# Batch 0's first loads cut at another place and put in another order, and its key-value products in one row

## The chip, the cores and the metric

The kernel runs on one core of a Trainium2 chip. What counts is the device time of one execution in microseconds. A core has five engines that work side by side, each through its own list of instructions: TensorE (PE; its weight loads stand as PEld), VectorE (DVE), ScalarE (ACT), GpSimd (POOL) and SyncE (SP, here only an issuer of transfers). Sixteen DMA engines move the data between the chip's main memory and the core's memory of 128 partitions.

## The reference

A linear attention over 8 batches, 8 heads, 576 tokens and 64 dimensions, with an RMS norm, feeds a mixture of 8 experts with soft slots (4 slots for each). All data are 32-bit floats.

```
kv  = einsum('bhsd,bhse->bhde', k, v)          # one 64x64 matrix per batch and head
out = einsum('bhsd,bhde->bhse', q, kv)
x   = out / sqrt(mean(out*out) + 1e-6) * g_norm    # 4608 tokens x 512
logits = x @ phi                                # 4608 x 32 slots
d = softmax(logits over tokens);  slot_input = d.T @ x
h = relu(slot_input[e] @ w1[e]);  slot_out[e] = h @ w2[e]      # 8 experts, 512x1024 and 1024x512
result = softmax(logits over slots) @ slot_out
```

Inputs are read once: keys, values and queries (28 MB) and the weights (34 MB); 9.4 MB are written.

## The kernel before, in words

Every operation is recorded first, with its engine, by a small planner (class `Order`), and then emitted in the recorded order for each engine; the planner only adds the waits. So the order of the calls in the function is the order of each engine's list, and all compute instructions show the planner's line, 215.

**Memory.** Loads go into one large array, `arena`: 144 columns at its head (phi and the norm's weights) and behind them a field of 160 blocks of 256 columns. `KV_AT`, `Q_AT` and `W_AT` give each piece its block. Batch 0's keys and values have block 0 (4608 columns: two halves of heads, `g` = 0 and 1, each 2048 columns of `kv_main` and 256 of `kv_rest`). Directly behind, at block 18, stands the q of batches 0 and 1 (`Q_AT[0]`): 2048 columns of `q_main` for batch 0, 2048 for batch 1, 512 of `q_rest` for the token tile that both share. Blocks are used again: the fourth batch's keys and values go to block 0 once batch 0's products have read it.

**Loads.** All go out on SP's queue, in order. Before, the first is the head and half `g` = 0 of batch 0; the second the half `g` = 1 and batch 0's `q_main`; the third batch 1's keys and values; the fourth the rest of that q; the fifth batch 2's keys and values with the next q. They are issued without any wait. The next three follow behind batch 0's products in the program, and the first of them waits until block 0 is free. Later loads (the last attention data, the experts' weights) are issued behind certain token tiles or experts, each when its place is free. The stores of the result use the same queue at the end.

**Attention.** `Kv` has for each batch `products` (64-column matmuls), `borders` (the last 64 tokens, and the copy of the products to `kvT` on ScalarE) and `slots` (transposes, the product with the norm-weighted phi, and the copies to `bd`, which is the weight side of what follows). For batch 0 the two halves of heads are worked off one after the other. Then the 36 token tiles (`T`) go by: `products(T)` multiplies q by `bd` on TensorE; ScalarE squares and evicts; VectorE and GpSimd norm, sum and scale. Batch 1's keys and values are multiplied (`kv_step(1, 0)`, `kv_step(1, 1)`) on TensorE right before tile 3, and its slots fall into tile 3; batch 2's come at tile 8 and before, and so on.

**Fills.** `fill` and `fill_wide` are matmuls whose result is never read. `EARLY` says how many stand at the start: five short ones (`fill`, 16-bit zeros, 512 columns), two wide ones (`fill_wide`, 32-bit ones, 512 columns) ahead of batch 0, one short in each half, and two wide ones behind the first half.

**Experts and output.** The softmax over tokens ends in `sTe`; then eight experts run, `expert_h` with `w1` and `expert_y` with `w2`, each behind its weights' loads, and the output is made in twelve chunks: chunks 0 to 5 behind the first half of the experts' second product, chunks 6 to 11 behind the second. The last store takes chunks 8 to 11 (3072 KB), the one before it chunks 6 and 7 (1536 KB).

Of the kernel before, what the change touches and what calls it, by code (L numbers as in the profile page):

```python
# [5 lines left out]
F32 = mybir.dt.float32  # L6
# [5 lines left out]
P = 128  # L12
B, H, S, D = 8, 8, 576, 64
# [9 lines left out]
CT = 12  # L23
NCH = NT // CT
NX = 14
EARLY = (5, 2, 0)
LATE_FILL = (4, 3, 3, 1, 1)
TOK = 4608
UNIT = 4096
# [3 lines left out]
KV_AT = (0, 36, 54, 0, 90, 126, 18, 54)  # L33
Q_AT = (18, 72, 108, 36)
# [27 lines left out]
SHARED = (5, 11)  # L62
BEHIND = {4: (2, 3), 5: (4, 5, 6, 7)}
HEAD = 144
SCRATCH = 1024
WORK = {
    "kvT": (1, 256), "sq": (2, 1024), "part": (3, 512), "ms": (3, 16), "r0": (2, 16), "r": (3, 16), "r1": (2, 16),
# [221 lines left out]
def soft_moe_linear_attention(nc, first_in, kv0_in, kv_in, q0_in, kv2_in, kv4_in, kv5_in, t3_in, w_in, out):  # L289
# [3 lines left out]
    wk = Pool({tag: [nc.sbuf([P, n], F32, f"{tag}{i}") for i in range(bufs)] for tag, (bufs, n) in WORK.items()})  # L293
    banks = nc.psum(8)
    arena = const.tile([P, HEAD + ARENA], F32, name="arena")
    phi_sb = arena[:, :128].rearrange("p (g w n) -> p g w n", g=2, w=2)
# [5 lines left out]
    def place(at, n):  # L302
        return arena[:, HEAD + at * KB : HEAD + at * KB + n]

    def load_row(at, src):
        nc.sync.dma_start(place(at, src.shape[-1]), src)
# [4 lines left out]
    def kv_rest(b, g):  # L311
        return place(KV_AT[b], TOK)[:, g * 2304 + 2048 : g * 2304 + 2304]
# [28 lines left out]
        return parts[k][:, at : at + 256]  # L341


    nc.sync.dma_start(arena[:, : HEAD + 2304], first_in)
    load_row(KV_AT[0] + 9, kv0_in)
    load_row(KV_AT[1], kv_in[0])
    load_row(Q_AT[0] + 8, q0_in)
    load_row(KV_AT[2], kv2_in)


# [47 lines left out]
    def pool(**tags):  # L398
        return Pool({tag: [flat_banks(banks, b, n) for b in at] for tag, (n, *at) in tags.items()})

    ps = pool(o=(2, 0, 2), kv=(2, 4), m=(1, 6), s=(1, 7))


    class Kv:
# [10 lines left out]
        def products(self, r):  # L415
            g, w = divmod(r, 2)
            main = kv_main(self.b, g).rearrange("p (r w c n) -> p r w c n", r=2, w=2, c=4)
            for c in range(4):
                for i in range(2):
                    lo = 64 * i  # L420
                    nc.tensor.matmul(
                        self.pkv[lo : lo + 64, w, g],
                        lhsT=main[:, w, 1, c, lo : lo + 64],
                        rhs=main[:, w, 0, c, lo : lo + 64],
                        start=c == 0 and (g == 0 or self.b == 0),
                        stop=False,
                    )

        def borders(self, gs):

            for g in gs:
                half = kv_rest(self.b, g).rearrange("p (w n) -> p w n", w=2)
                for i in range(2):
                    for w in range(2):
                        lo, at = 64 * i, 64 * w
                        nc.tensor.matmul(
                            self.pkv[lo : lo + 64, w, g],
                            lhsT=half[at : at + 64, 1, lo : lo + 64],
                            rhs=half[at : at + 64, 0, lo : lo + 64],
                            start=False,  # L440
                            stop=g == gs[-1],
                        )
            n = len(gs)
            self.kvT = wk.tile([P, n, 2, D], F32, tag="kvT", name=f"kvT{self.b}_{gs[0]}", bufs=1)
            nc.scalar.copy(self.kvT, self.pkv[:, :, gs[0] : gs[0] + n].rearrange("p w g d -> p g w d"))

        def slots(self, gs):
# [211 lines left out]
    first = {b: 9 * (b // 2) + 4 * (b % 2) for b in range(B)}  # L659
# [8 lines left out]
    def kv_step(b, i):  # L668
        if i == 0:
            kvs[b] = Kv(b)  # L670
            kvs[b].products(0)
            kvs[b].products(1)
        elif i == 1:
            kvs[b].products(2)
            kvs[b].products(3)
            kvs[b].borders((0, 1))
        else:
            kvs[b].slots((0, 1))
# [9 lines left out]
    def fill(n, cols=256, home=None):  # L688

        if not n:  # L690
            return
        t = home if home is not None else ps.tile([P, 2, 512], F32, tag="o", name="fill", bufs=2)[:, 1]
        for i in range(n):
            nc.tensor.matmul(
                t[:, :cols].rearrange("p (a n) -> p a n", n=256),
                lhsT=zeros[:, :P],
                rhs=zeros.unsqueeze(1).to_broadcast([P, cols // 256, 256]),
                start=True,
                stop=True,
            )  # L700

    def fill_wide(t, n):
        for i in range(n):
            nc.tensor.matmul(
                t.rearrange("p (a n) -> p a n", n=P),
                lhsT=ones,
                rhs=ones.unsqueeze(1).to_broadcast([P, 4, P]),
                start=True,
                stop=True,
            )  # L710

    fill(EARLY[0], cols=512)
    fill_wide(ps.tile([P, 512], F32, tag="m", name="fill"), 2)

    for g in range(2):
        kv = Kv(0, "o" if g else "kv", 2 if g else None)
        kv.products(2 * g)
        kv.products(2 * g + 1)
        kv.borders((g,))
        fill(1, cols=512)  # L720
        kv.slots((g,))
        fill_wide(ps.tile([P, 512], F32, tag="m", name="fill"), EARLY[1 + g])
    load_row(KV_AT[3], kv_in[1])
    load_row(Q_AT[1] + 8, kv4_in)
    load_row(Q_AT[2], kv5_in)
# [1 line left out]
    for T in range(NT - 2):  # L727
# [4 lines left out]
        o = products(T, (lambda: kv_step(late[0], 2)) if late else None)  # L732
# [110 lines left out]
    ps = pool(y=(2, 0), m=(2, 2, 4, 6))  # L843
# [182 lines left out]
def build_program():  # L1026
    import concourse.bacc as bacc

    nc = bacc.Bacc("TRN2", target_bir_lowering=False, num_devices=1, dynamic_dma_scratch_size=SCRATCH)
    shapes = {  # L1030
        "first": (P, HEAD + 2304), "kv0": (P, 2304 + 2048), "kv": (2, P, TOK), "q0": (P, 2560),
        "kv2": (P, TOK + 2048),
        "kv4": (P, 2560 + TOK), "kv5": (P, 2 * TOK), "t3": (P, 3 * TOK),
        "w": (1, 2 * NE * P * UNIT),
    }
    args = [nc.dram_tensor(f"in_{n}_dram", s, F32, kind="ExternalInput").ap() for n, s in shapes.items()]
    args.append(nc.dram_tensor("out_0_dram", (1, 4 * NCH * P * 4 * CT * NS), F32, kind="ExternalOutput").ap())
    order = Order(nc)
    soft_moe_linear_attention(order, *args)
    order.emit()  # L1040
    return nc
# [62 lines left out]
```

## Time and profile before

| | |
|---|---|
| runs (device us) | 171.58, 171.75, 244.36; median 171.75 |
| profiled execution | 171.73 us, its span 170.4 us |
| busy in the span | PE 151.0, PEld 104.0, DVE 86.9, ACT 88.5, POOL 59.6 us |
| moved | 71.65 MB, 421 GB/s over the span |

The time of an execution is a little longer than its span, which runs from the first to the last instruction. Busy time is the time in which an engine has an instruction at work. A transfer has an issue (on SP's list), packets on the sixteen DMA engines, and a landing, when the waiting engines may go on. The share of DMA is the mean busy share of the sixteen engines; packets that overlap in the records can carry it a little above 1.

### The profile page before, as it was taken

How to read it: one execution, taken by the hardware profiler on the slowest of the kernel's cores; microseconds unless marked ns; L12 is line 12 of the kernel's file. 1: busy time of each engine (PE TensorE's matmuls, PEld its weight loads, DVE VectorE, ACT ScalarE, POOL GpSimd, SP SyncE). 2: the span in 40 equal slices, each digit the busy share in tenths (PEclk: the TensorE clock that was granted, in tenths of full speed). 3: DMA queues.
4: the chain of work that ended last, by engine and by line, in shares of the span. 5: the costliest groups of instructions: out<-in, count | busy, mean ns of one | idle time of the engine just before them, and what ended most of it. 6: DMA issues, size and time to landing. Idle time of an engine off the chain costs nothing.

```text
span 170.4 us, 4234 instructions
## 1 busy us (share of the span) xinstructions
PE 151.0 (89%) x1834; PEld 104.0 (61%) x1834; DVE 86.9 (51%) x185; ACT 88.5 (52%) x230; POOL 59.6 (35%) x73
## 2 busy tenths in 40 slices
PE   7998998999999899999899989989999989989200
PEld 3457987979688888796696664345566533454000
DVE  1111437743677265763936798724888036319300
ACT  3015778786965887768849864202234044418300
POOL 7000247757356755366482589300000004000000
PEclk9999999999999999999999999999999999999855
DMA  5999999999999999999999999999999999999996
GB/s 193 440 435 417 478 413 409 457 430 478 419 415 439 432 441 413 419 400 460 400 458 408 448 408 423 431 458 396 431 427 431 452 435 396 427 415 439 415 447 288
DMA packets 3933, 71.65 MB, mean 421 GB/s; under 512 B 742, under 2 KB 742, under 8 KB 874
## 3 DMA queue, kind: packets, MB, share of 16 engines
q1 hardware_dynamic: 3562, 71.18, 97.8%
q8 instruction: 14, 0.23, 0.5%
q0 software_dynamic: 352, 0.20, 0.4%
q14 instruction: 5, 0.04, 0.1%
HBM read 61.94 MB, written 9.44 MB: 419 GB/s over the span
## 4 chain that ended last, share of the span: by engine, by line
PE 54%; DMA 16%; ACT 15%; DVE 6%; issue 1%; SPq 0%
PE psum L215 54%; DMA arena<-in_w_dram 10%; DMA arena<-in_kv_dram 6%; ACT bd L215 4%; ACT sq L215 4%; ACT xall L215 2%; DVE ms L215 2%; DVE logits L215 1%; ACT part L215 1%; ACT arena L215 1%; ACT r L215 1%; ACT d L215 1%; DVE part L215 1%; DVE acc L215 1%; DVE r L215 0%
## 5 line engine op out<-in xcount | busy, mean ns | idle before, releaser
L215 PE MATMUL psum<-bd,arena 128*128 128x192 f32 (+1 forms) x320 | 56.6, 336 | 2.4 <-ACT bd L215 1.2
L215 PEld LDWEIGHTS psum<-bd,arena 128*128 128x128 f32 (+1 forms) x320 | 45.5, 179 | 9.7 <-ACT xall L215 3.5
L215 DVE TENSOR_REDUCE ms<-sq 128x16 f32<-128x1024 f32 (+1 forms) x19 | 22.1, 1162 | 28.6 <-ACT sq L215 28.5
L215 POOL TENSOR_TENSOR part<-part,r 128x512 f32<-128x512 f32 x17 | 17.8, 1047 | 48.9 <-DVE r L215 48.9
L215 POOL TENSOR_TENSOR xall<-xall,r 128x512 f32<-128x512 f32 x34 | 34.7, 1042 | 0.0
L215 ACT ACTIVATE sq<-psum 128x512 f32<-128x512 f32 x36 | 21.5, 596 | 9.0 <-PE psum L215 8.9
L215 PEld LDWEIGHTS psum<-arena 128*64 128x64 f32 (+1 forms) x640 | 18.8, 137 | 6.6 <-issue 3.0
L215 PE MATMUL psum<-arena 128*64 128x64 f32 (+1 forms) x640 | 21.4, 226 | 0.3 <-DMA arena<-in_kv_dram 0.3
L215 ACT COPY xall<-psum 128x512 f32<-128x512 f32 x34 | 20.7, 608 | 0.0
L215 ACT COPY part<-psum 128x256 f32<-128x256 f32 (+1 forms) x38 | 13.7, 359 | 9.2 <-DVE part L215 8.0
L215 DVE TENSOR_REDUCE logits<-part 128x64 f32<-128x512 f32 (+1 forms) x18 | 17.8, 991 | 0.0
L215 PE MATMUL psum<-arena,xall 128*32 128x256 f32 x256 | 15.0, 380 | 0.4 <-DMA arena<-in_w_dram 0.4
L215 DVE COPY arena<-psum 128x768 f32<-128x768 f32 (+1 forms) x12 | 10.5, 889 | 6.8 <-PE psum L215 6.8
L215 ACT COPY arena<-psum 128x768 f32<-128x768 f32 (+1 forms) x14 | 10.2, 754 | 7.1 <-PE psum L215 7.1
L215 PE MATMUL psum<-logits,part 32*128 32x384 f32 x96 | 12.7, 527 | 0.6 <-ACT arena L215 0.4
L215 POOL DMA_DIRECT2D out_dram<-arena x2 | 1.2, 589 | 33.8 <-DVE arena L215 33.8
L215 PE MATMUL psum<-arena,sq 128*32 128x256 f32 x224 | 12.7, 379 | 0.2 <-DVE sq L215 0.2
L215 PEld LDWEIGHTS psum<-arena,xall 128*32 128x32 f32 x256 | 8.1, 110 | 6.9 <-issue 1.4
L215 PE MATMUL psum<-xall,d 128*32 128x258 f32 x144 | 10.8, 390 | 1.0 <-ACT d L215 1.0
L215 ACT COPY bd<-psum 64x128 f32<-64x128 f32 (+1 forms) x32 | 9.8, 308 | 2.4 <-PE psum L215 2.2
L215 PEld LDWEIGHTS psum<-arena,sq 128*32 128x32 f32 x224 | 7.2, 110 | 5.1 <-DVE sq L215 0.5
L215 ACT COPY kvT<-psum 128x256 f32<-128x256 f32 (+1 forms) x9 | 3.1, 348 | 12.6 <-PE psum L215 12.5
(80 smaller groups left out, 129.7 us busy)
## 6 DMA issues: line engine op xcount, KB each, us to landing
arena<-in_w_dram SPq DMA_DIRECT2D x4, 4096.0 KB, 23.8
arena<-in_w_dram SPq DMA_DIRECT2D x4, 2048.0 KB, 20.5
arena<-in_t_dram SPq DMA_DIRECT2D x1, 6912.0 KB, 35.6
arena<-in_w_dram SPq DMA_DIRECT2D x2, 3072.0 KB, 22.9
arena<-in_kv_dram SPq DMA_DIRECT2D x2, 2304.0 KB, 19.0
arena<-in_kv_dram SPq DMA_DIRECT2D x1, 4608.0 KB, 40.3
arena<-in_kv_dram SPq DMA_DIRECT2D x1, 3584.0 KB, 29.9
arena<-in_kv_dram SPq DMA_DIRECT2D x1, 3328.0 KB, 26.0
```

The lines of the kernel that those rows point to most:

```text
L215: inst = getattr(engine, method)(*args, **kwargs)
```

## The change

The same bytes come in four transfers again, cut at other places. The first one holds the head and the start of batch 0's keys and values, 512 columns (2048 bytes a row). The second holds the rest of batch 0's keys and values, both halves, 4240 columns. The third is the whole q of batches 0 and 1, 4608 columns, and the fourth batch 1's keys and values. Ahead of batch 0 stand now five short fills, five wide and one short. Batch 0's products are worked off in one row: the first half's products, half of the second's, then the slots of the first half, the rest of the second, its slots, and one wide fill. The copy `kvT` of a half goes to its own part of the tile.

```diff
-EARLY = (5, 2, 0)
+EARLY = (5, 5, 1, 1)
+AHEAD = 512
-    nc.sync.dma_start(arena[:, : HEAD + 2304], first_in)
-    load_row(KV_AT[0] + 9, kv0_in)
+    nc.sync.dma_start(arena[:, :AHEAD], first_in)
+    nc.sync.dma_start(arena[:, AHEAD : HEAD + TOK], kv0_in)
+    load_row(Q_AT[0], q0_in)
     load_row(KV_AT[1], kv_in[0])
-    load_row(Q_AT[0] + 8, q0_in)
     load_row(KV_AT[2], kv2_in)
...
-            self.kvT = wk.tile([P, n, 2, D], F32, tag="kvT", name=f"kvT{self.b}_{gs[0]}", bufs=1)
+            self.kvT = wk.tile([P, 2, 2, D], F32, tag="kvT", name=f"kvT{self.b}_{gs[0]}", bufs=1)[:, gs[0] : gs[0] + n]
...
     fill(EARLY[0], cols=512)
-    fill_wide(ps.tile([P, 512], F32, tag="m", name="fill"), 2)
-
-    for g in range(2):
-        kv = Kv(0, "o" if g else "kv", 2 if g else None)
+    wide = ps.tile([P, 512], F32, tag="m", name="fill")
+    fill_wide(wide, EARLY[1])
+    fill(EARLY[2], home=wide, cols=512)
+
+    halves0 = [Kv(0, "o" if g else "kv", 2 if g else None) for g in range(2)]
+    for g, kv in enumerate(halves0):
         kv.products(2 * g)
+        if g:
+            halves0[0].slots((0,))
         kv.products(2 * g + 1)
         kv.borders((g,))
-        fill(1, cols=512)
-        kv.slots((g,))
-        fill_wide(ps.tile([P, 512], F32, tag="m", name="fill"), EARLY[1 + g])
+    halves0[1].slots((1,))
+    fill_wide(ps.tile([P, 512], F32, tag="m", name="fill"), EARLY[3])
     load_row(KV_AT[3], kv_in[1])
...
-        "first": (P, HEAD + 2304), "kv0": (P, 2304 + 2048), "kv": (2, P, TOK), "q0": (P, 2560),
+        "first": (P, AHEAD), "kv0": (P, HEAD + TOK - AHEAD), "kv": (2, P, TOK), "q0": (P, TOK),
```

The host lays the input arrays out to match; nothing else is changed.

## Rows read from the trace of the kernel before

**Rows 1.** The page: busy time by engine, and strips of 40 slices in tenths.
```profile
PE 151.0 (89%) x1834; PEld 104.0 (61%) x1834; DVE 86.9 (51%) x185; ACT 88.5 (52%) x230; POOL 59.6 (35%) x73
...
PEclk9999999999999999999999999999999999999855
DMA  5999999999999999999999999999999999999996
```

**Rows 2.** Busy time by stage: stretch, engines, granted TensorE clock, DMA share, GB/s.
```profile
0.00:1.76 1.76, 0.70 (x2) 0.28 (x3) 0.58 (x3) 1.02 (x1) 0.88 (x8) 1.00 0.00 0
1.76:3.00 1.24, 1.24 (x4) 0.55 (x3) 0.15 (x1) 0.26 (x1) 1.03 (x3) 1.00 0.87 205
3.00:5.00 2.00, 2.00 (x4) 0.86 (x4) 0.00 (x0) 0.00 (x0) 1.10 (x4) 1.00 1.03 436
30.00:60.00 30.00, 29.12 (x406) 24.71 (x408) 17.72 (x37) 23.07 (x64) 18.29 (x18) 1.00 1.02 437
...
158.80:160.50 1.70, 0.00 (x0) 0.00 (x0) 0.55 (x1) 0.48 (x1) 0.00 (x0) 1.00 1.00 426
160.60:162.00 1.40, 0.00 (x0) 0.00 (x0) 0.00 (x0) 0.00 (x0) 0.00 (x0) 0.50 1.05 448
```

**Rows 3.** Waits of PE: total us, times, longest us.
```profile
PE psum L215 <- DMA arena<-in_w_dram: 0.4, 1, 0.4
```

**Rows 4.** Order of time on SP's list (start, us): first issues, last two stores.
```profile
0.74 0.38 SPq L215 DMA_DIRECT2D arena<-in_first_dram  x1
...
1.18 0.42 SPq L215 DMA_DIRECT2D arena<-in_kv_dram  x1
...
1.64 0.43 SPq L215 DMA_DIRECT2D arena<-in_kv_dram  x1
2.12 0.64 SPq L215 DMA_DIRECT2D arena<-in_q_dram  x1
...
155.28 0.34 SPq L215 DMA_DIRECT2D out_dram<-arena  x1
...
159.42 0.33 SPq L215 DMA_DIRECT2D out_dram<-arena  x1
```

**Rows 5.** DMA issues: times, KB each, us from issue to landing (the median).
```profile
arena<-in_first_dram SPq DMA_DIRECT2D x1, 1224.0 KB, 5.3
...
arena<-in_kv_dram SPq DMA_DIRECT2D x1, 2176.0 KB, 10.0
...
arena<-in_kv_dram SPq DMA_DIRECT2D x1, 2304.0 KB, 16.4
...
arena<-in_q_dram SPq DMA_DIRECT2D x1, 1280.0 KB, 18.8
...
arena<-in_w_dram SPq DMA_DIRECT2D x4, 4096.0 KB, 23.8
...
out_dram<-arena SPq DMA_DIRECT2D x1, 1536.0 KB, 7.8
...
out_dram<-arena SPq DMA_DIRECT2D x1, 3072.0 KB, 10.9
```

**Rows 6.** PE in order of time: start, us, operation, records, idle before.
```profile
1.06 2.31 PE L215 MATMUL psum<-zeros 128*128 128x512 bf16 x5 [1.06 <-DVE zeros L215]
3.17 3.62 PE L215 MATMUL psum<-ones 128*128 128x512 f32 x4
6.71 1.52 PE L215 MATMUL psum<-arena 128*64 128x64 f32 x40
...
9.01 1.88 PE L215 MATMUL psum<-ones 128*128 128x512 f32 x4
...
13.97 4.58 PE L215 MATMUL psum<-bd,arena 128*128 128x192 f32 x24 [0.40 <-ACT bd L215]
18.48 2.48 PE L215 MATMUL psum<-arena 128*64 128x64 f32 x80
...
102.44 1.52 PE L215 MATMUL psum<-xall,d 128*32 128x258 f32 x24 [0.81 <-ACT d L215]
```

More of the change, by code (lines that the diff above doesn't have):

```diff
@@ L1076 @@
     rows = [np.concatenate([w[k] for k in row], axis=1).reshape(-1) for row in W_ROWS]
-    first = np.zeros((P, HEAD + 2304), np.float32)
+    first = np.zeros((P, HEAD + TOK), np.float32)
     first[:, :129] = cs
-    first[:, HEAD:] = kv[0, :, :2304]
+    first[:, HEAD:] = kv[0]
     arrays = {
-        "in_first_dram": first,
-        "in_kv0_dram": np.concatenate([kv[0, :, 2304:], qm[0][:, :2048]], axis=1),
+        "in_first_dram": np.ascontiguousarray(first[:, :AHEAD]),
+        "in_kv0_dram": np.ascontiguousarray(first[:, AHEAD:]),
         "in_kv_dram": np.ascontiguousarray(kv[1:4:2]),
-        "in_q0_dram": np.ascontiguousarray(qm[0][:, 2048:]),
+        "in_q0_dram": qm[0],
         "in_kv2_dram": np.concatenate([kv[2], qm[1][:, :2048]], axis=1),
```

## Prediction

> **What bounds the kernel now.** I read the strip of the page first [rows 1]. It shows two resources that are both nearly full: TensorE is busy for 89% of the span, and the DMA engines for nine tenths or more of every slice between the first and the last. So I asked for the busy time by stage [rows 2]. From 3 us on the sixteen DMA engines have a busy share of 1.0 and more and move 426 to 448 GB/s, also after 158.8 us, where TensorE has stopped. TensorE is busy for 29.1 us out of 30 in the middle of the attention part. Neither waits much for the other: behind the first microseconds PE waits for a transfer only once, 0.4 us for weights [rows 3].
>
> Which of the two sets the end? The last store (3072 KB) is issued at 159.42 us and lands 10.9 us later, at 170.3; the store ahead of it (1536 KB) is issued at 155.28 and lands 7.8 us later, at 163.1 [rows 4, 5]. Between these landings lie 7.24 us, and 3.146 MB in 7.24 us is 434 GB/s, the full rate. So the last store ran without a gap behind the one before: it stood in a queue, and **the transfers set the end**. The weight loads show the same from the other side: 4.19 MB at 427 GB/s are 9.8 us of work, yet such a load lands 23.8 us after its issue (median) [rows 5]. The others have a backlog of well over 10 us ahead of them. Lateness of TensorE costs nothing as long as it does not empty that queue.
>
> The profiled execution took 171.73 us, 1.33 more than its span, and stands at the median of 171.75. I add to the median.
>
> **The change, part by part.** *The bytes.* Before, the first load, the second, batch 1's keys and values and the rest of q are 1224 + 2176 + 2304 + 1280 = 6984 KB [rows 5]. After, 256 + 2120 (batch 0's keys and values) + 2304 (q) + 2304 (batch 1) = 6984 KB, again four transfers of 128 rows. The stream gets no longer and no shorter. The rows grow smaller at one place (2 KB). The bulk rate is the same with 9.8 KB rows (436 GB/s at 3 to 5 us) and with the larger ones behind it [rows 2], so 128 short rows are costed at zero within the ramp below.
>
> *The ramp.* No packet starts before 1.76 us, 1.02 us after the first issue; from 1.76 to 3.00 the rate is 205 GB/s instead of 436 [rows 2, 4]. That moves 254 KB of 541 and loses 0.66 us. If the ramp costs a time, the new one costs the same; if it costs a number of packets, it is over with fewer bytes moved (up to 0.66 us worse) or with shorter packets (up to 0.66 better). I take 0, since the second load is issued 0.44 us behind the first [rows 4] and about 254 KB, all of the new first load, is what the ramp carries by 3.00 us, so the second can be there at its end.
>
> [...]
>
> *Batch 0 on TensorE.* The two halves now start together behind the second load. Before, 1224 + 2176 KB are there at 11.2 us; now 2376 KB are, some 2.4 us earlier, at about 8.8. But TensorE comes later than that: five short fills, then five wide ones that show as two records each. [...] Four at 0.90 from 3.17 and six at 0.47 end at 9.6, and the sixth short fill, at most 0.5 (five took 2.31), by about 10.0. Then come 40 product records (1.5), 16 (0.6), the first half's slots (0.4), 24 records (0.9), copy and slots of the second half (0.8, as from 8.23 to 9.01 before; the slots are about half of that) and one wide fill of two records (0.9): the first token product starts at about 15.1 instead of 13.97 [rows 6]. The q that it needs has landed by then: 4680 KB stand at 11.2 + 2.9 = 14.1 us, by the 2.9 us that the 1280 KB took (18.04 to 20.92) [rows 4, 5]. [...]
>
> The 1.1 us are covered by a later wait. Before token tile 3 TensorE multiplies batch 1's keys and values, at 18.48 [rows 6]. Before, these had landed at 1.64 + 16.4 = 18.04; now they stand behind 1280 KB more, where the late q load landed: 2.12 + 18.8 = **20.92** [rows 4, 5]. Tiles 0 to 2 take 13.97 to 18.48, 4.5 us, so TensorE reaches the wait at 19.6, idles 1.3 us and goes on at 20.92: 2.44 us later than before. Behind it on TensorE stands tile 3; ScalarE, VectorE and GpSimd, fed by it, move along. With 29.1 busy us out of 30 [rows 2] nothing is left in the attention part to catch up with.
>
> *The other queues.* SP still issues four transfers for these bytes; batch 1's is now the fourth instead of the third and goes out 0.5 us later, behind a queue that holds it anyway. SP issues the next three loads behind batch 0's last product (its first buffer is reused), about 1 us later than before; the loads queued ahead of them last beyond 20.92. Later loads are issued 2.4 us later against a backlog of over 10. GpSimd's queue is not touched.
>
> *The expert part and the tail.* There TensorE waits 0.4 us for a weight load that comes with the stream [rows 3], and the delay falls to 2.03 us. The last store is issued at 161.45 instead of 159.42. Is its data still in time? Counting from the first load, the engines need 1.02 us from issue to the first packet, and, with what the ramp moves counted at full rate, 1.68 us of effective delay (2.26 less 254 KB at 436 GB/s). So it starts effectively at 162.5 to 163.1. The store ahead lands at 163.08; by the first load, which has its 1.25 MB moved by about 5.3 and lands at 6.04 [rows 2, 4, 5], a landing trails its bytes by up to 0.75 us. The hole is therefore 0 to 0.8 us; I take 0.4, the middle, as no row is nearer to one end. **Sum: 171.75 + 0 (bytes) + 0 (ramp, -0.66 to +0.66) + 0.4 (tail, 0 to 0.8), or 172.1 us.**
>
> **The rivals.**
> *A, the queue is no cushion.* If the stores start later after their issue than loads do, the 2.03 us reach the end whole: 173.8 us. For it: TensorE is as full as the engines are, and the last store's lead is only about 2 us. Against it: 434 GB/s between the last landings. Chance 0.10.
>
> *B, the clock falls in the new wait, the case that ends slower than before.* The row shows that at the end TensorE stopped at 158.8, was still granted 1.00 up to 160.50 and 0.50 from 160.60 [rows 2]. So a halt of 1.7 us did cost the higher level, and the new one at tile 3 has 1.3 us. If it falls, TensorE works at half speed for about as long as at the start (1.06 to 6.7 us), and loses half of 5.7 us, 2.85; past the tail's cushion that counts whole: 172.1 + 2.85 = 175.0 us. It decides once the halt comes to about 1.7 us, that is, if the fills end 0.4 us earlier than I sum up. Against it, the halt of 0.81 us at 102.44 [rows 6] has no dip of the clock in the page's strip of tenths [rows 1]. [...] Chance 0.10.
>
> *C, the short first load leaves the engines idle.* The first load needs 5.3 us from issue to landing for 2.9 us of bytes. If these 2.4 us were not hidden by the load behind it, the stream would end that much later: 174.1 us. Against it, the issues follow at 0.44 us. Chance 0.05. [...]
>
> *D, the ramp gets cheaper.* 0.66 us less and no hole at the end: 171.1 us. Small packets could pass the start-up sooner. Chance 0.12.
>
> **How the numbers follow.** My forecast, 172.1 us (171.5 to 173.2 by the bounds of ramp and tail), has the other 0.63. The range is 171.1 to 174.2: it takes in D's end, A and C, and leaves out B and a little on each side. A measurement of this kernel can tell about 2% (3.4 us) from no change, thus 168.3 and 175.2 us. No case reaches 168.3, and 0.02 stands for what I do not see; half of B may pass 175.2 if the low clock lasts longer than at the start, so 0.06 for slower and 0.92 for the same.
>
> **What would show it.** The load of batch 1 lands near 20.9 and PE shows a wait for it at tile 3 of 0.5 to 2 us; the tiles behind run some 2.4 us late; the wait for weights at 134 us is gone; the last store is issued near 161.4 and still lands near 170.5; the DMA share stays at 1.0 from 3 us on. A granted clock below 1.00 after 20 us would show B; a DMA share below 0.9 between 2 and 5 us, C. I am wrong if TensorE's delay is made up somewhere that shows no idle time before, or if the stores turn out to be issued too late to keep the queue full.

## The result and the profile after

| | before | after |
|---|---|---|
| median (lowest to highest) | 171.75 us (171.58 to 171.93 but for one disturbed run) | 172.93 us (172.22 to 173.76) |
| ratio after to before | | 1.0069, 95% interval 1.0045 to 1.0092 |
| profiled execution, its span | 171.73, 170.4 us | 172.93, 171.6 us |

The change makes the kernel slower by 0.7%, 1.18 us in the medians, and its runs scatter over 1.5 us instead of 0.35. It stays within 2%. The disturbed run of before took 244.36 us and is left out of the ratio.

The page after, busy time and the strip of DMA, answers to [rows 1]:

```profile
PE 151.9 (89%) x1837; PEld 105.1 (61%) x1837; DVE 87.0 (51%) x185; ACT 88.5 (52%) x230; POOL 59.7 (35%) x73
...
DMA  5999999999999998999999999999999999999994
```

Little in it tells the two kernels apart at this grain. The order of time does. The PE list after, from the first fill to batch 1's products (answers to [rows 6]; the last row ends at 22 us and holds 26 of the 80 records):

```profile
3.16 6.39 PE L216 MATMUL psum<-ones 128*128 128x512 f32 x10
9.38 0.38 PE L216 MATMUL psum<-zeros 128*128 128x512 bf16 x1
9.69 2.04 PE L216 MATMUL psum<-arena 128*64 128x64 f32 x56
...
14.76 4.55 PE L216 MATMUL psum<-bd,arena 128*128 128x192 f32 x24
21.20 0.98 PE L216 MATMUL psum<-arena 128*64 128x64 f32 x26 [1.90 <-DMA arena<-in_kv_dram]
```

The loads after, KB and us from issue to landing (answers to [rows 5]); their issues stand at 0.74, 1.19, 1.65 and 2.12 us:

```profile
arena<-in_first_dram SPq DMA_DIRECT2D x1, 256.0 KB, 2.8
...
arena<-in_kv_dram SPq DMA_DIRECT2D x1, 2120.0 KB, 8.0
...
arena<-in_q_dram SPq DMA_DIRECT2D x1, 2304.0 KB, 13.0
...
arena<-in_kv_dram SPq DMA_DIRECT2D x1, 2304.0 KB, 19.0
```

Batch 0 is there 2 us earlier, at 9.2 us, and TensorE could not use it before 9.69. Batch 1 is there at 2.12 + 19.0 = 21.1 us instead of 18.0, and TensorE, which came to its products at 19.3, stands still for 1.90 us. They begin 2.72 us later than before (21.20 to 18.48). At the other end, the last two stores on SP's list and their landing (answers to [rows 4, 5]):

```profile
157.25 0.34 SPq L216 DMA_DIRECT2D out_dram<-arena  x1
...
161.39 0.33 SPq L216 DMA_DIRECT2D out_dram<-arena  x1
```

```profile
out_dram<-arena SPq DMA_DIRECT2D x1, 3072.0 KB, 10.2
...
out_dram<-arena SPq DMA_DIRECT2D x1, 1536.0 KB, 7.1
```

Both are issued 1.97 us later than before and land 1.2 us later, at 164.3 and 171.6. The weight loads' wait of 0.4 us [rows 3] is gone, as it took most of the rest of the delay: the row of 102.44 us [rows 6], ahead of that wait, now starts at 105.04, 2.60 us later.

### The profile page after: what moved, and what is told of

The parts are those of the page before. It is cut to its first block, busy times and chain, and to the rows that moved or that the text cites. A ratio compares the mean times of both kernels' runs of the same rounds, so it can differ in the third digit from the quotient of the medians.

```text
span 171.6 us, 4242 instructions
## 1 busy us (share of the span) xinstructions
PE 151.9 (89%) x1837; PEld 105.1 (61%) x1837; DVE 87.0 (51%) x185; ACT 88.5 (52%) x230; POOL 59.7 (35%) x73
## 4 chain that ended last, share of the span: by engine, by line
PE 61%; ACT 14%; DMA 11%; DVE 6%; issue 1%; SPq 1%
PE psum L216 61%; DMA arena<-in_kv_dram 11%; ACT bd L216 4%; ACT sq L216 3%; DVE ms L216 2%; ACT xall L216 2%; DVE logits L216 1%; ACT part L216 1%; ACT arena L216 1%; ACT r L216 1%; ACT d L216 1%; SPq L216 1%; DVE part L216 1%; DVE acc L216 1%; DVE r L216 0%
## 5 line engine op out<-in xcount | busy, mean ns | idle before, releaser
L216 PE MATMUL psum<-ones 128*128 128x512 f32 x20 | 11.1, 703 | 0.0
```

The source lines that it names most:

```text
L216: inst = getattr(engine, method)(*args, **kwargs)
```

## The experiments

Two theories first. **L (late):** batch 1's later landing makes TensorE late, the stores follow, and the tail does not absorb all of it. **R (ramp):** the short rows of the first load start some DMA engines badly, and the stream is uneven to its end. Four kernels part L and R.

**Order undone.** The changed kernel, with batch 1 third again:

```diff
-    load_row(Q_AT[0], q0_in)
+    load_row(Q_AT[0], q0_in[:, :2048])
     load_row(KV_AT[1], kv_in[0])
+    load_row(Q_AT[0] + 8, q0_in[:, 2048:])
```

> The changed kernel, but its q load is cut in two (2048 columns of batch 0, then the rest) and batch 1's keys and values go between them, third as before; TensorE's wait at tile 3 should be gone. Theory L (the wait makes the last stores about 2 us late, and that costs the 1.2 us): 171.6 to 171.9 us. Theory R (the short first rows start some DMA engines late, and these carry it to the end): 172.3 to 173.0 us, with runs scattered over a microsecond.

Measured: 171.83 us, ratio 1.0005 (0.9996 to 1.0013), eleven runs within 0.3 us. The loss and the scatter are gone, with the short first load and batch 0 in one row still in place. The last store is issued at 159.54 us.

**Order alone.** The kernel before, with these two loads exchanged:

```diff
-    load_row(KV_AT[1], kv_in[0])
     load_row(Q_AT[0] + 8, q0_in)
+    load_row(KV_AT[1], kv_in[0])
```

> The kernel before with one thing changed: the loads of batch 1's keys and values and of the rest of q change places, so TensorE waits near 21 us for batch 1. The first two loads stay. Theory L: 172.3 to 173.0 us, as slow as the changed kernel. Theory R: 171.7 us, as before.

Measured: 173.62 us, ratio 1.0085 (1.0057 to 1.0113). The order alone brings all of the loss and more, 1.89 us in the medians against 1.18. But the eight times fall into two groups: 172.29 to 172.33 (three) and 173.53 to 173.94 (five). The trace is from the lower group; it shows a halt of 2.37 us ahead of batch 1's products and the last store at 161.28.

**Short first load alone:**

```diff
-    nc.sync.dma_start(arena[:, : HEAD + 2304], first_in)
+    nc.sync.dma_start(arena[:, :512], first_in[:, :512])
+    nc.sync.dma_start(arena[:, 512 : HEAD + 2304], first_in[:, 512:])
```

> The kernel before with one thing changed: its first load is cut into one of 512 columns (2048 bytes a row) and one of the rest; the order of all else stays, and TensorE's work too. Theory R: 172.2 to 173.0 us, scattered. Theory L: 171.7 us, as before.

Measured: 171.60 us, ratio 0.9991 (0.9983 to 1.0000). No loss, so R falls; if anything a gain of 0.13 us, which the repeat below did not confirm.

**Lateness alone.** No load is changed; fills ahead of tile 3 make TensorE late without letting it stand still:

```diff
     for T in range(NT - 2):
+        if T == 3:
+            fill_wide(ps.tile([P, 512], F32, tag="m", name="fill"), 3)
```

> The kernel before with no load changed, but three wide fills (six records of 0.43 us, 2.6 us) ahead of batch 1's products at tile 3, so TensorE is late by as much as in the changed kernel, without an idle wait. Theory L: 172.3 to 173.0 us. Theory R: 171.7 us. If it lies between, lateness is a part of the loss only.

Measured: 172.37 us, ratio 1.0031 (1.0020 to 1.0042). The last store is issued at 161.44, as late as in the changed kernel, and all seven runs lie between 171.96 and 172.47. So lateness costs 0.5 to 0.6 us: L holds for about half of the loss. The other half, and the wider scatter, appear so far only where TensorE is late because it stands still.

That gave a third theory, **C (clock)**: in a part of the runs TensorE's granted clock falls in the idle wait, as it does from 1.00 to 0.50 behind the end of its work [rows 2], and these are the times of the upper group. The runs that follow part C from L, and measure by its dose the cushion, that is, how much lateness the queue of stores absorbs.

**The wait filled.** The changed kernel, with fills in the place of the halt:

```diff
     for T in range(NT - 2):
+        if T == 3:
+            fill_wide(ps.tile([P, 512], F32, tag="m", name="fill"), 2)
```

> The changed kernel with two wide fills (four records, 1.7 us) ahead of batch 1's products at tile 3, in the place of its idle wait of 1.9 us; TensorE goes on at the same time, but has not stood still. Theory L (lateness alone): 172.2 to 173.8 us and as scattered as the changed kernel. Theory C (in part of the runs the clock falls in the idle wait, and these are the runs near 173.5): 172.2 to 172.5 us, close together, as the late kernel with fills and no changed load (172.4).

Measured: 172.38 us, ratio 1.0044 (1.0028 to 1.0059), six runs from 172.24 to 172.97. Batch 1's products begin at 21.18 us, as in the changed kernel, behind fills that leave a wait of 0.18, and the last store goes out at 161.38, the same time too. The runs above 173 are missing, five of eleven in the changed kernel. It points to C; but six runs are few, and the intervals of the two ratios still overlap.

**One more trace of the exchanged loads**, to catch a time of the upper group:

> The kernel before with batch 1's load in fourth place once more, for one more trace of it. Its eight times lay at 172.3 (three) and 173.5 to 173.9 (five). Theory C: if this run is one of the slow ones, the trace shows a granted clock of 0.50 for some microseconds behind the wait at 21 us, and tiles that come later than in the quick run. Theory L: the clock stays at 1.00 and the difference arises at the end.

Measured: 172.30 us, the lower group, with a halt of 2.60 us, behind which the 80 records take 2.48 us as without a halt, and a mean granted clock of 0.977, as in the short runs. It tells nothing of the upper one.

**A smaller and a double dose** in the kernel before, against the three fills above:

```diff
-            fill_wide(ps.tile([P, 512], F32, tag="m", name="fill"), 3)
+            fill_wide(ps.tile([P, 512], F32, tag="m", name="fill"), 1)    # and 6
```

> The kernel before with one wide fill (two records, 0.9 us) ahead of tile 3. If the tail has a cushion of about 2 us: 171.7 us, as before. If the late stores cost in proportion (0.64 us for 2.6): 171.9 to 172.0.

Measured: 171.72 us, ratio 0.9998 (0.9989 to 1.0006), last store at 159.69 (0.27 us late).

> The kernel before with six wide fills (5.2 us) ahead of tile 3. Past the cushion each microsecond counts whole: 172.4 + 2.6 = 174.9 us, or 174.6 if TensorE gets a part back at the wait for weights. In proportion: 173.0 us. If the transfers alone set the end: 171.7.

Measured: 174.83 us, ratio 1.0179 (1.0160 to 1.0198), last store at 164.15 (4.73 us late). There is a cushion, and past it lateness counts nearly whole: 2.02 us late cost 0.64 in the medians and 4.73 late cost 3.10, so that 1.4 to 1.6 us are absorbed.

**A longer halt, and the same filled.** 512 KB of the fifth load go ahead of batch 1's in the exchanged order:

```diff
     load_row(Q_AT[0] + 8, q0_in)
+    load_row(KV_AT[2], kv2_in[:, :1024])
     load_row(KV_AT[1], kv_in[0])
-    load_row(KV_AT[2], kv2_in)
+    load_row(KV_AT[2] + 4, kv2_in[:, 1024:])
```

> The kernel before with batch 1's load in fourth place and 512 KB of the next load pulled ahead of it, so it lands near 22.2 us and TensorE stands still for some 3.7 us at tile 3. The stores come 3.3 us late, and with a cushion of about 1.5 us (from 2.0 us late for 0.64 and 4.7 us late for 3.10) lateness alone gives 173.5 us. Theory C: the clock falls in this longer halt in all runs, its record shows 0.50 behind 20 us, and the time is 174.3 to 175.2 us.

Measured: 174.84 us, ratio 1.0207 (1.0165 to 1.0249), four runs from 174.15 to 176.21. The same loads with fills ahead of tile 3:

```diff
+        if T == 3:
+            fill_wide(ps.tile([P, 512], F32, tag="m", name="fill"), 4)
```

> The same order of loads, with four wide fills (eight records, 3.4 us) in the place of the halt. TensorE goes on at the same time. Both theories: 173.5 us (173.2 to 173.8), clock at 1.00; the difference to the kernel with the halt is the price of the clock alone.

Measured: 173.10 us, ratio 1.0084 (1.0065 to 1.0103), four runs from 172.81 to 173.74. The filled one is 0.4 us under what both theories gave: 3.18 us late (last store at 162.60) for 1.38, so here the cushion took 1.8. The two differ by 1.74 us in the medians for the same loads, and the traced executions by 1.18 (174.15 to 172.97); the last store goes out at 163.86 with the halt, 1.26 later than with the fills. The traced execution with the halt is the shortest of its four. For it the trace shows the cause. PE in order of time, with the halt:

```profile
17.80 0.81 PE L215 MATMUL psum<-bd,arena 128*128 128x192 f32 x4
22.20 3.70 PE L215 MATMUL psum<-arena 128*64 128x64 f32 x80 [3.58 <-DMA arena<-in_kv_dram]
25.83 1.18 PE L215 MATMUL psum<-bd,arena 128*128 128x192 f32 x4
26.84 0.38 PE L215 MATMUL psum<-ident,kvT 128*128 128x128 f32 x2
```

and with the fills:

```profile
18.51 3.60 PE L215 MATMUL psum<-ones 128*128 128x512 f32 x8
22.39 2.48 PE L215 MATMUL psum<-arena 128*64 128x64 f32 x80 [0.28 <-DMA arena<-in_kv_dram]
24.79 0.92 PE L215 MATMUL psum<-bd,arena 128*128 128x192 f32 x4
25.55 0.38 PE L215 MATMUL psum<-ident,kvT 128*128 128x128 f32 x2
```

The 80 records take 3.70 us behind the halt and 2.48 behind the fills, and what follows them comes 1.29 us later although they began 0.19 earlier. The windows with the halt give the clock (third number from the end):

```profile
21.00:22.00 1.00, 0.00 (x0) 0.00 (x0) 0.00 (x0) 0.00 (x0) 1.00 (x2) 1.00 0.93 401
22.00:23.00 1.00, 0.81 (x26) 0.81 (x28) 0.00 (x0) 0.00 (x0) 1.00 (x2) 0.99 1.04 451
23.00:24.00 1.00, 1.00 (x26) 1.00 (x24) 0.00 (x0) 0.00 (x0) 0.14 (x1) 0.50 1.25 541
24.00:25.00 1.00, 1.00 (x24) 1.00 (x21) 0.00 (x0) 0.00 (x0) 0.00 (x0) 0.50 0.94 406
25.00:26.00 1.00, 1.00 (x23) 0.77 (x20) 0.00 (x0) 0.04 (x1) 0.00 (x0) 0.50 0.89 383
26.00:27.00 1.00, 1.00 (x6) 0.98 (x7) 0.00 (x0) 0.34 (x1) 0.00 (x0) 0.81 0.88 379
```

TensorE goes on at 22.2, still at 1.00; about 0.8 us later the granted clock falls to 0.50 (0.99 over 22 to 23 us, 0.50 over 23 to 24), and it is back between 26 and 27 us (0.81). With the fills the same column has 1.00 from 21 to 29 us. A halt of 3.58 us did it here in the run that was traced, and the fall came 0.8 us after the work had begun again.

**Two repeats.**

> The kernel before with its first load cut at 512 columns, once more, to see if the 0.13 us by which it was ahead (171.60 to 171.73) come again on another chip. If they are real: 171.5 to 171.7 us; if not: 171.7 to 171.8.

Measured: 171.70 us, ratio 0.9999 (0.9990 to 1.0008). The gain of the short first load is not there on another chip; no version here beats the kernel before.

> The changed kernel once more, for one more trace. Its eleven times reached from 172.2 to 173.8 us. Theory C: a run above 173 shows a granted clock of 0.50 behind the wait at 21 us; a run near 172.3 does not.

Measured: 172.62 us, with the clock at 1.00 behind its halt of 1.89 us (windows from 21 to 29 us and 30 to 60). This too was a run without the fall.

## Why the prediction came out as it did

It said 172.1 us for a reason, and the measured 172.93 lies in its range; the sign and the path up to the stores were right, and the size of the loss was three times the 0.4 us that I had summed up. One bound in it is a slip: by the bounds of ramp and tail the forecast reaches down to 171.75 - 0.66 = 171.1 us, not 171.5.

*The bytes and the ramp.* Right, at zero. The windows after, answers to [rows 2], show another shape and the same sum:

```profile
1.76:3.00 1.24, 1.24 (x4) 0.56 (x3) 0.15 (x1) 0.26 (x1) 1.03 (x3) 1.00 0.85 311
3.00:5.00 2.00, 2.00 (x4) 0.88 (x4) 0.66 (x2) 0.00 (x0) 1.15 (x4) 1.00 0.96 370
```

311 x 1.24 + 370 x 2 = 1126 KB by 5 us, and before 205 x 1.24 + 436 x 2 = 1126 KB (in units of 1000 bytes). The kernel with only the short first load, 171.60 and 171.70 us, confirms it. So the prediction's rivals C (engines left idle) and D (a cheaper ramp) did not happen. A load of 256 KB cost nothing where the next one is issued 0.45 us behind: 171.60 and 171.70 us with it, 171.73 and 171.72 for the kernel before beside them.

*Batch 0 and the wait at tile 3.* Right in kind, with small errors. The fills were through by 9.7 us instead of 10.0, and the first token product came at 14.76 instead of 15.1. The ten records of the wide fills took 6.39 us, as four of 0.90 and six of 0.47 do (6.4), the lengths that [rows 6] give (3.62 us for four early, 1.88 us for four at 9.01); why the early ones are longer, no run shows. The wait was 1.90 us instead of 1.3, since TensorE came to it 0.3 us earlier (19.3) and batch 1 landed 0.2 us later than the row that stood for it.

*Nothing to catch up with, and the expert part.* Right: of 2.72 us, 1.97 reach the last store (I had 2.03 out of 2.44). The wait for weights took some 0.6 us instead of 0.41 (2.60 us late ahead of it). The fills show the same lateness with no load changed (2.02).

*The tail is the step that was mis-sized.* I gave it 0.4 us (0 to 0.8), from one hole in front of the last store. The lateness alone measures 0.53 to 0.75 us, by the kernels with fills, and the last store landed at 171.6 instead of near 170.5. No hole in front of it shows: the last two landings lie 7.2 us apart before (163.1 to 170.3) and after (164.3 to 171.6). I had looked at the last store only, and the traced loss is there two stores earlier. Issue, and us to landing, of the 2304 KB store, before:

```profile
148.75 0.36 SPq L215 DMA_DIRECT2D out_dram<-arena  x1
...
out_dram<-arena SPq DMA_DIRECT2D x1, 2304.0 KB, 10.7
```

After:

```profile
150.74 0.36 SPq L216 DMA_DIRECT2D out_dram<-arena  x1
...
out_dram<-arena SPq DMA_DIRECT2D x1, 2304.0 KB, 9.9
```

It lands at 159.5 and at 160.6. All three stores go out 2 us late, and the DMA engines move less from 144 to 163 us. Before:

```profile
144.00:149.00 5.00, 5.00 (x80) 2.36 (x80) 2.13 (x3) 1.98 (x3) 0.00 (x0) 1.00 1.00 416
149.00:158.00 9.00, 8.06 (x90) 4.42 (x84) 4.85 (x7) 4.54 (x8) 0.00 (x0) 1.00 1.01 420
158.00:163.00 5.00, 0.76 (x4) 0.14 (x4) 0.89 (x2) 0.97 (x2) 0.00 (x0) 0.76 1.06 451
163.00:166.00 3.00, 0.00 (x0) 0.00 (x0) 0.00 (x0) 0.00 (x0) 0.00 (x0) 0.50 0.99 426
166.00:169.00 3.00, 0.00 (x0) 0.00 (x0) 0.00 (x0) 0.00 (x0) 0.00 (x0) 0.50 0.97 418
```

After:

```profile
144.00:149.00 5.00, 5.00 (x54) 2.26 (x57) 2.77 (x3) 2.23 (x3) 1.67 (x3) 1.00 0.97 388
149.00:158.00 9.00, 8.26 (x108) 4.41 (x100) 3.59 (x6) 4.06 (x8) 0.00 (x0) 1.00 1.00 413
158.00:163.00 5.00, 2.53 (x18) 1.20 (x16) 2.71 (x4) 2.63 (x4) 0.00 (x0) 1.00 1.00 429
163.00:166.00 3.00, 0.00 (x0) 0.00 (x0) 0.00 (x0) 0.00 (x0) 0.00 (x0) 0.67 1.05 451
166.00:169.00 3.00, 0.00 (x0) 0.00 (x0) 0.00 (x0) 0.00 (x0) 0.00 (x0) 0.50 1.06 459
```

Before with three fills, late by 2.02 us:

```profile
144.00:149.00 5.00, 5.00 (x54) 2.26 (x57) 2.82 (x3) 2.28 (x3) 1.71 (x3) 1.00 0.99 402
149.00:158.00 9.00, 8.26 (x108) 4.41 (x100) 3.54 (x6) 4.01 (x8) 0.00 (x0) 1.00 1.00 415
158.00:163.00 5.00, 2.59 (x18) 1.20 (x16) 2.76 (x4) 2.68 (x5) 0.00 (x0) 0.87 1.00 426
163.00:166.00 3.00, 0.00 (x0) 0.00 (x0) 0.00 (x0) 0.00 (x0) 0.00 (x0) 0.50 1.03 442
166.00:169.00 3.00, 0.00 (x0) 0.00 (x0) 0.00 (x0) 0.00 (x0) 0.00 (x0) 0.50 1.04 451
```

Read the last column. Up to 163 us after moves 28 GB/s less than before over 5 us, 7 less over 9 and 22 less over 5: 140 + 63 + 110 = 313 KB. From 163 to 169 us it moves 25 and 41 GB/s more, 75 + 123 = 198 KB, so that 115 KB are left, 0.3 us at 434 GB/s. With the fills 240 KB are missing at 163 us and 93 KB at 169, 0.2 us. So the mean over the engines accounts for about a quarter of the 1.2 us of the traced run and of the 0.8 us of the traced run with fills.

The rest is in the last engines to finish. A trace records sixteen landings of the last store, as many as there are DMA engines. The middle of the sixteen comes at 169.96 us before, 170.18 after and 170.13 with the fills; the last of them at 170.34, 171.56 and 171.11. Lateness of the stores is what the fills add, so it makes the last landings late; why only a few of the sixteen, no run here shows.

*Rival B was half right, and it can hold for a part of the rest only.* I gave it 0.10, with a price of 2.85 us in every run and a threshold of 1.7 us of halt. The threshold did not hold: halts of 1.90 and 1.89 us left the clock at 1.00 (windows from 21 to 26 us in both traces), and with 2.37 and 2.60 us the mean granted clock was 0.979 and 0.977, no lower than in the other short runs. The loss beyond lateness (172.93 to 172.38 in the medians) goes away when the halt is filled, at the same lateness. Yet the traced run at that very median, 172.93, and the second trace, 172.62, had the clock at 1.00 behind the halt and the last store out at 161.39 and 161.40, as the kernel with three fills (161.44, traced at 172.47). What is later in them is the last of the sixteen landings (171.56 and 171.25 to 171.11), and its cause is open.

The clock is left for the five runs above 173 and for the upper group of the exchanged loads, 1.2 to 1.7 us over the lower one. The mean granted clock that is on record for every run goes with this: 0.977 to 0.979 in the three short runs of the exchanged loads and 0.967 to 0.971 in the five long ones; 0.973 to 0.978 up to 172.93 in the changed kernel and 0.968 to 0.972 above 173; 0.971 in the two short runs of the longer halt and 0.962 in the two long ones (175.44 and 176.21). This agrees with C but is no proof of it. The kernel before has 0.968 to 0.979 in runs of 171.5 to 172.2 us, since the mean also holds the low clock behind the end of TensorE's work (0.50 from 160.60 us [rows 2]), and the two longest runs of the changed kernel with its wait filled (172.75 and 172.97) have its lowest, 0.972 and 0.971.

So in the longer halt the fall of the clock is shown; in the changed kernel it is argued only, since both of its traces (halts of 1.90 and 1.89 us) and both of the exchanged loads (2.37 and 2.60) fell on runs without it. The forecast had the halt at 1.3 us; at 1.9 a part of the runs may lose the clock, and so B should have had more than a tenth. Its price was too high: in the longer halt the clock was low from about 23 to 26.4 us, not for the 5.7 us that I had taken from the start. No run shows a low clock there: it was my estimate from the length of the early records (0.90 us against 0.47 [rows 6]), and the clock column has 1.00 at 1.76 to 5 us [rows 2].

*Rival A* (no cushion, 173.8 us) is excluded by the dose: a last store that is 2.02 us late costs a third of that.

## What to carry to other kernels

Where the transfers bound a kernel from end to end, an order of loads is worth what it does to the engine that feeds the last stores: put ahead what is needed first (batch 1's keys and values), and behind what is needed later (batch 1's q), even at the price of one more transfer (171.83 us). Work out the cushion at the tail over all late stores and by the slowest engine to finish, not from the last store, the mean rate or the busy share. And a halt of TensorE can cost a second time through the clock, as the one of 3.58 us did; fills in its place are the test, and here the cheaper form of the same lateness (173.10 to 174.84 us).

## What the runs showed of the hardware that was not expected

The clock fell late and not in the halt: TensorE stood still for 3.58 us, took up work at 22.2 us with the granted clock at 1.00, and was set to 0.50 only at about 23 (0.99 over 22 to 23 us, 0.50 over 23 to 24), in the middle of 80 dense records. Halts of 1.89, 1.90, 2.37 and 2.60 us passed without a fall in the runs that were traced (1.00 from 21 to 26 us behind the first two, mean granted clocks of 0.979 and 0.977 in the other two), while the end of TensorE's work was followed by a fall after 1.7 us in the kernel before (1.00 from 158.80 to 160.50 us, 0.50 from 160.60 [rows 2]): the length of the halt alone did not decide.
